# Recurrence and expert layer on one core: reordered first steps, and the last four tiles' lists built in two parts

## The chip, the cores and the metric

The kernel runs on one core of one Trainium2 chip. The metric is the device time of one execution in microseconds (us), the median of several runs. The engines are TensorE (PE; its weight loads are a row of their own, PEld), VectorE (DVE), ScalarE (ACT), GpSimd (POOL) and SyncE (SP), which here only issues transfers. Each works through its own instructions in order; the program fixes that order, and an instruction that waits holds all that stand behind it on its engine.

## What is computed

A recurrence over 768 positions for 4 batches of 8 heads of width 48, and then a layer of 8 experts on the 3072 rows that it gives:

```python
for t in range(S):
    cur = einsum('bhd,bhe->bhde', u * k[t], v[t])
    y[t] = einsum('bhd,bhde->bhe', r[t], state + cur)
    state = w * state + einsum('bhd,bhe->bhde', k[t], v[t])
x = y as rows (3072 x 384)
do_compute = x @ w_skip > 0
logits = x[do_compute] @ w_gate          # 8 experts
e_idx = argmax(logits); gate = softmax(logits)[e_idx]
out[row] = x[row] + gate * (relu(x[row] @ w1[e]) @ w2[e])   # rows not chosen: x
```

## The kernel before, in words

**The recurrence** runs in 24 steps n = 0 to 23: two pairs of batches, 12 steps each, every step 64 positions of two batches. A step's r is multiplied by a table of powers of w (`prep_r`, on VectorE), its k by a table of inverse powers (`prep_k`, mostly on POOL); a second copy of r, the bonus, carries u (`bonus`: one part per pair of heads on ScalarE, or a half at once on another engine). There are four such tables, `w_d[0..3]`; `grow(1)`, `grow(2)`, `grow(3)` make the later ones from the first. On TensorE a step is `scores` (k times r), `within` (masked scores times v), `turn_x` and `turn_k` (transposes), `state` and `across`. `mask_scores(n)` copies the scores out of the bank `ps_p` in two VectorE operations; the scores of step n+1 go into the same bank. `warm` puts matmuls without use on TensorE while it has nothing else. `blank` zeroes the part of a v tile that a block-diagonal product needs empty.

`load_rk(n)` brings r and k of a step, `load_v` its v. All loads are issued by SP, except `ub` and k of step 0, which ScalarE issues. The order of the first steps is written out by hand (lines 959 to 981).

**Routing.** A step's 128 rows are a tile. Gating gives each tile 9 logits in `lg`; tiles 0 to 22 are gated by fours (`gate_four`, `gate_back`), tile 23 alone (`gate`, line 692). `route` turns the logits of a group of tiles into lists, for each expert, of row numbers and weights: groups (0, 8), (8, 16), (16, 20) and (20, 24). On VectorE it finds the maximum, the choice `oh`, the weight; on TensorE the ranks (line 770 and on), which need `oh`; on VectorE two operands `ol` and `vl`; on TensorE the list matmuls (line 842). Their result is added to `lists`; `place` makes the index `gid` from it, and `gather` brings the rows of the output that the index names, by a DMA from POOL. There are 16 slots of rows: slot 0 to 7 the first 128 rows of each expert, slot 8 to 15 up to 104 more. Slot 8 is the first one that the last group's lists are needed for.

**From attention to the experts.** Expert 0's slot 0 is worked on while the last steps run, by the generator `single` (called `first`; line 198): three groups of widening matmuls for one half of the hidden layer (line 218), then the other half, `flip` (transposes and a copy), `narrow` (line 247) and `rest` (the low part, on VectorE). `run(k)` lets it go on by k pieces. After the last step come lines 1077 to 1087: one piece, the gating of tile 23, the routing of the last group up to its choice, two pieces, the ranks and the operands, two pieces, lists and index; then the gathers. Slot 8 is the next slot that TensorE turns, while it still works on slot 0. After that, experts 1 to 7 follow in `expert`.

Of the kernel before, what the change touches and what calls it, by code (L numbers as in the profile page):

```python
# [9 lines left out]
F32 = mybir.dt.float32  # L10
F32R = mybir.dt.float32r
# [11 lines left out]
P = 128  # L23
# [38 lines left out]
def tile_wkv_moe(  # L62
# [135 lines left out]
    def single(q, w1, w2, xhl, made, ph, pt, py, turned=False):  # L198
# [69 lines left out]
        if turned:  # L268
            rest(0)
            narrow(0, 1, parts=(0,))  # L270
            yield
            flip(1)
            narrow(2, 3, parts=(0,))
            narrow(0, 1, 2, 3, parts=(1,))
            rest(1)
        else:
            narrow(0, 1)
            yield
            flip(1)
            rest(1)  # L280
            narrow(2, 3)
# [12 lines left out]
    with ExitStack() as actx:  # L294
# [34 lines left out]
        def load_rk(n):  # L329
            d = ld.tile([DR, 2, NB * NHP * C], F32, tag="dm", name=f"dm{n}", bufs=3)  # L330
            for eng, s in ((nc.sync, slice(0, 1)), (nc.scalar, slice(1, 2))) if n == 0 else ((nc.sync, slice(0, 2)),):
                eng.dma_start(
                    out=d[:, s].rearrange("p s (q c) -> p s q c", c=C), in_=dm[n // NSTEP, n % NSTEP, :, s]
                )
            loaded[n] = (d, v_of(n))
# [377 lines left out]
        def route(g0, g1):  # L713
# [4 lines left out]
            def near(w=None):  # L718
                if g1 == NT:
                    free[0] += 1  # L720
                    return small(f"near{free[0]}", w=w, bufs=1)
                a = free[0]
# [25 lines left out]
            nc.vector.tensor_tensor(df, l8, bc(mx), ALU.subtract)  # L748
            if g1 == NT:
                nc.scalar.activation(df, df, AF.Exp)  # L750
            yield 0
            if g1 < NT:
                nc.scalar.activation(df, df, AF.Exp)
            nc.vector.tensor_tensor(eq[:, :, :E], eq[:, :, :E], rdo, ALU.mult)
# [72 lines left out]
            if late:  # L827
                nc.vector.tensor_tensor(
                    ol, lane1[:, None, :].to_broadcast([P, n, P]), r1.unsqueeze(2).to_broadcast([P, n, P]), ALU.is_equal
                )  # L830
                ohp = oh
                if g1 < NT:
                    ohp = near(E)
                    nc.vector.tensor_copy(ohp, oh)
                vl = small("vl", F32R, NV3 * E)
# [10 lines left out]
                nc.vector.tensor_tensor(last, part[:, :, NJ - 1, :], last, ALU.add)  # L846
                if g1 < NT:
                    count()
                    nc.vector.tensor_tensor(before, before, sums, ALU.add)
                else:  # L850
                    place(1)
                nc.vector.tensor_scalar(over[:, g0:g1], r1, float(CAP), None, ALU.is_ge)
# [39 lines left out]

        def place(j):
            c = slice(j * E, (j + 1) * E)
            ids = lists[:, 0, j]
            nc.vector.tensor_scalar(gid[:, c], ids, 1.0, 0.0, ALU.subtract, ALU.max)
            em2 = sm.tile([P, E], F32, tag="em2", name=f"em2{j}")
# [71 lines left out]
        square(8, nc.gpsimd)  # L969
        k1 = prep_k(1, after=prep_r(1))  # L970
        for j in range(2, 4):
            blank(j, nc.gpsimd)
        bonus(1, (0, 1, 2, 3))
        mask_scores(0)
        warm(3, ps_t)
        state(0)
        warm(2, ps_t)
        grow(2, nc.vector)
        prep_k(2, after=prep_r(2))
        bonus(2, (0, 1, 2, 3))  # L980
        grow(3, nc.gpsimd)

# [90 lines left out]
        def run(k):  # L1073
            for _ in range(k):
                next(first, None)

        run(1)
        gate(NT - 1)
        assert not routes
        last = route(ends[NT], NT)  # L1080
        while next(last) == 0:
            pass
        run(2)
        while next(last) == 0:
            pass
        run(2)
        both(last)
# [341 lines left out]
```

## Time and profile before

| | us |
|---|---|
| median of 3 runs | 266.14 |
| lowest and highest run | 264.6, 269.08 |
| profiled execution, its own time | 263.44 |
| span of the profiled execution, first to last instruction | 261.7 |
| mean granted TensorE clock | 0.996 |
| TensorE busy in the span | 252.4 (96%) |
| VectorE, ScalarE, POOL busy | 169.6, 139.0, 112.6 |

Times in the trace count from the start of the span. The steps of the recurrence fill the first 115 us or so, the experts the time from about 136 us on. Busy shares are means over stretches with different limits; what a change is worth is read from the waits in its own stretch.

### The profile page before, as it was taken

How to read it: one execution, taken by the hardware profiler on the slowest of the kernel's cores; microseconds unless marked ns; L12 is line 12 of the kernel's file. 1: busy time of each engine (PE TensorE's matmuls, PEld its weight loads, DVE VectorE, ACT ScalarE, POOL GpSimd, SP SyncE). 2: the span in 40 equal slices, each digit the busy share in tenths (PEclk: the TensorE clock that was granted, in tenths of full speed). 3: DMA queues.
4: the chain of work that ended last, by engine and by line, in shares of the span. 5: the costliest groups of instructions: out<-in, count | busy, mean ns of one | idle time of the engine just before them, and what ended most of it. 6: DMA issues, size and time to landing. Idle time of an engine off the chain costs nothing.

```text
span 261.7 us, 8596 instructions
## 1 busy us (share of the span) xinstructions
PE 252.4 (96%) x3578; PEld 225.2 (86%) x3580; DVE 169.6 (65%) x381; ACT 139.0 (53%) x315; POOL 112.6 (43%) x130
## 2 busy tenths in 40 slices
PE   7999999999999999999999999999999999999990
PEld 2688888888887888778699999999999999999990
DVE  7867547579554696638873797858569387494300
ACT  2655766667656664635753837539167273490200
POOL 7679647476646836202887061310501303105011
PEclk9999999999999999999999999999999999999998
DMA  6998699989998688695499959394390760001000
GB/s 170 252 248 253 207 259 257 270 223 277 234 255 230 170 261 272 146 326 182 130 301 294 324 168 367 114 357 170 100 407 13 260 271 29 19 0 40 7 33 24
DMA packets 20704, 51.82 MB, mean 198 GB/s; under 512 B 3540, under 2 KB 9952, under 8 KB 20656
## 3 DMA queue, kind: packets, MB, share of 16 engines
q1 hardware_dynamic: 18352, 45.81, 58.6%
q0 software_dynamic: 2048, 5.14, 6.3%
q8 instruction: 30, 0.49, 0.8%
q10 hardware_dynamic: 256, 0.23, 0.3%
q14 instruction: 18, 0.15, 0.2%
HBM read 43.77 MB, written 7.96 MB: 198 GB/s over the span
## 4 chain that ended last, share of the span: by engine, by line
PE 95%; DMA 1%; issue 1%; DVE 1%; POOL 0%; POOLq 0%; ACT 0%
PE ps_p L179 11%; PE ps_y L179 11%; PE ps_p L533 9%; PE ps_y L587 8%; PE ps_s L557 7%; PE ps_p L169 5%; PE ps_y L169 5%; PE ps_x L169 5%; PE ps_l L169 5%; PE ps_y L603 5%; PE ps_t L657 4%; PE ps_l L519 3%; PE ps_t L304 3%; PE ps_t L674 2%; PE ps_y L247 2%; PE ps_l L218 2%
## 5 line engine op out<-in xcount | busy, mean ns | idle before, releaser
L188 POOL DMA_INDIRECT out_dram<-xg,sid x16 | 24.8, 1550 | 88.3 <-DVE xg L184 78.4
L130 DVE TENSOR_TENSOR wlo<-raw,whi 128x512 fp32r<-128x512 f32 x84 | 53.9, 683 | 1.3 <-ACT h L222 0.7
L125 ACT CAST whi<-raw 128x512 fp32r<-128x512 f32 x96 | 54.7, 627 | 0.0
L506 POOL TENSOR_TENSOR kd<-dm,w_d 112x512 f32<-112x512 f32 x23 | 29.3, 1275 | 2.1 <-DVE rd L481 2.0
L139 POOL DMA_INDIRECT xg<-out_dram,gid x16 | 19.2, 1200 | 20.0 <-DVE em L898 15.7
L481 DVE TENSOR_TENSOR rd<-dm,w_d 112x512 f32<-112x512 f32 x24 | 17.3, 722 | 14.9 <-PE ps_y L603 14.0
L533 PE MATMUL ps_p<-rd,kd 48*64 48x128 f32 x768 | 26.8, 274 | 0.0
L491 POOL TENSOR_TENSOR rd<-rd,uw 112x256 f32<-112x256 f32 x21 | 12.9, 613 | 30.5 <-DVE rd L481 15.3
L533 PEld LDWEIGHTS ps_p<-rd,kd 48*64 48x64 f32 x768 | 21.1, 133 | 2.6 <-issue 1.2
L545 DVE COPY_PREDICATED am<-below,ps_p 128x512 f32<-128x512 int8 x24 | 17.7, 737 | 6.7 <-PE ps_p L533 6.3
L587 PE MATMUL ps_y<-vkv,am 128*64 128x96 f32 x384 | 21.4, 253 | 0.6 <-issue 0.6
L499 ACT ACTIVATE rd<-rd,uw 112x128 f32<-112x128 f32 x52 | 17.9, 396 | 7.3 <-DVE rd L481 7.1
L661 ACT COPY x<-ps_t 128x384 f32<-128x384 f32 x23 | 11.0, 479 | 19.1 <-PE ps_t L657 19.0
L587 PEld LDWEIGHTS ps_y<-vkv,am 128*64 128x64 f32 x384 | 16.7, 136 | 4.9 <-issue 3.5
L173 ACT ACTIVATE hh<-ps_p 128x464 fp32r<-128x464 f32 x7 | 3.9, 558 | 31.1 <-PE ps_p L169 31.1
L179 PE MATMUL ps_p<-whi,hh 128*128 128x384 f32 x56 | 19.4, 347 | 0.0
L557 PE MATMUL ps_s<-vkv,kt 128*48 128x96 f32 x352 | 19.1, 251 | 0.0
L179 PE MATMUL ps_y<-whi,hh 128*104 128x384 f32 x56 | 18.9, 338 | 0.0
L179 PE MATMUL ps_y<-wlo,hh 128*104 128x384 f32 x56 | 18.9, 337 | 0.0
L179 PE MATMUL ps_p<-whi,hl 128*128 128x384 f32 x56 | 18.9, 337 | 0.0
L179 PE MATMUL ps_y<-whi,hl 128*104 128x384 f32 x56 | 18.9, 337 | 0.0
L179 PE MATMUL ps_p<-wlo,hh 128*128 128x384 f32 x56 | 18.9, 337 | 0.0
(244 smaller groups left out, 610.6 us busy)
## 6 DMA issues: line engine op xcount, KB each, us to landing
raw<-in_w_dram SPq DMA_DIRECT2D x16, 768.0 KB
dm<-in_dm_dram SPq DMA_DIRECT2D x23, 448.0 KB
raw<-in_w_dram SPq DMA_DIRECT2D x24, 256.0 KB
raw<-in_w_dram SPq DMA_DIRECT2D x12, 512.0 KB
out_dram<-xt SPq DMA_DIRECT2D x24, 192.0 KB
vkv<-in_tok_dram SPq DMA_DIRECT2D x22, 192.0 KB
vkv<-in_tok_dram SPq DMA_DIRECT2D x4, 96.0 KB
out_dram<-xt SPq DMA_DIRECT2D x4, 96.0 KB
```

The lines of the kernel that those rows point to most:

```text
L125: nc.scalar.copy(wsp[e][0][:, s], raw[e][:, s])
L130: eng.tensor_tensor(lo[:, s], raw[e][:, s], hi[:, s].bitcast(F32), ALU.subtract)
L139: ins = nc.gpsimd.indirect_dma_start(out=xg[:m], out_offset=None, in_=out[:rows], in_offset=bass.IndirectOffsetOnAxis(ap=gid[:m, q : q + 1 ...
L169: nc.tensor.matmul(ph, w1[a][:, c, fs], x[:, c, b, :], start=(k == 0), stop=(k == 3 * NCC - 1))
L179: nc.tensor.matmul(py, a, b[:, f, :], start=(k == 0), stop=(k == 3 * NFC - 1))
L188: ins = nc.gpsimd.indirect_dma_start(out=out, out_offset=bass.IndirectOffsetOnAxis(ap=sid[:m, q : q + 1], axis=0), in_=xs.pop(q)[:m], in_o ...
L499: nc.scalar.activation(rd[:, :, hp, 1], rd[:, :, hp, 0], AF.Copy, scale=uw[:, hp : hp + 1])
L506: ins = (eng or nc.gpsimd).tensor_tensor(kds[n].rearrange("p b h c -> p b (h c)")[:, part], d[:, part], table.to_broadcast([DR, part.stop ...
L533: mm = nc.tensor.matmul(ps_p[g * C : (g + 1) * C, a, j * P : (j + 1) * P], kd[h, b, hp, :], rd[h, b, hp].rearrange("p s c -> p (s c)"), st ...
L545: nc.vector.copy_predicated(shape(am[n % 2]), below, p[:, :, 0])
L557: nc.tensor.matmul(s[a * C : a * C + D, j * 2 * D : (j + 1) * 2 * D], kt[:, j, a, :], v[:, j, a], start=i == 0 and j == 0, stop=True, skip ...
L587: nc.tensor.matmul(ps_y[b * C : (b + 1) * C, a, jj * 2 * D : (jj + 1) * 2 * D], am[n % 2][:, a, j * C : (j + 1) * C], v[:, j, a], start=jj ...
```

## The change

Four edits. (1) k of step 0 is issued by SP, right behind r, and no longer by ScalarE. (2) In the first three steps the bonus of steps 1 and 2 is made half by ScalarE and half by VectorE; the table of step 2 and k of step 2 come ahead of the mask of step 0; the two blocks that POOL zeroes stand apart; two of the five warming matmuls go. (3) The last group's routing is a function of its own, `route_end`. It chooses, ranks and spreads tiles 20 to 22 ahead of the gating of tile 23, then tile 23 alone, and makes the index straight from the bank in which the list matmuls leave their sums, ahead of the addition to `lists`. (4) `single` has one pause fewer, so that the first narrowing matmuls come behind the list matmuls. `route` loses the branches that only the last group used.

```diff
@@ single
         if turned:
             rest(0)
             narrow(0, 1, parts=(0,))
-            yield
             flip(1)
@@ load_rk
-            for eng, s in ((nc.sync, slice(0, 1)), (nc.scalar, slice(1, 2))) if n == 0 else ((nc.sync, slice(0, 2)),):
-                eng.dma_start(
+            for s in (slice(0, 1), slice(1, 2)) if n == 0 else (slice(0, 2),):
+                nc.sync.dma_start(
@@ route_end (new)
+            def choose(a, b):
+                q, l8, m = slice(a, b), lg[:, g0 + a : g0 + b, 0:E], b - a
+                nc.vector.tensor_reduce(mx[:, q], l8, AX.X, ALU.max)
+                nc.vector.scalar_tensor_tensor(rdo[:, q], ..., ALU.is_gt, ALU.mult)
+                nc.vector.tensor_tensor(eq[:, q, :E], l8, bc(mx[:, q]), ALU.is_equal)
+                nc.vector.tensor_tensor(df[:, q], l8, bc(mx[:, q]), ALU.subtract)
+                nc.scalar.activation(df[:, q], df[:, q], AF.Exp)
+                nc.vector.tensor_tensor(eq[:, q, :E], eq[:, q, :E], rdo[:, q], ALU.mult)
+                nc.vector.tensor_reduce(m2[:, q], eq[:, q], AX.X, ALU.max)
+                nc.vector.tensor_tensor(oh[:, q], eq[:, q, :E], bc(m2[:, q]), ALU.is_equal)
+            def rank(a, b):
+                nc.tensor.matmul(cols(0), tri, oh[:, a:b].rearrange(col), start=True, ...)
+                more = [(0, before[:, None, :].to_broadcast([P, m, E]))]
+                more += [(j, oh[:, a : b - j].rearrange(col)) for j in range(1, m)]
+                more += [(0, oh[:, j : j + 1].to_broadcast([P, m, E])) for j in range(a)]
+                for k, (j, x) in enumerate(more):
+                    nc.tensor.matmul(cols(j), ones[:, :P], x, start=False, ...)
+            def spread(a, b):
+                # on VectorE: sum of df, value of the row number, 1e-9, reciprocal, rank product,
+                # gh, its sum r1, gl, ol, value of gh, value of gl
...
+            choose(0, n - 1)
+            yield
+            rank(0, n - 1)
+            spread(0, n - 1)
+            nc.vector.tensor_scalar(ids1, lists[:, 0, NJ - 1], 1.0, 0.0, ALU.subtract, ALU.max)
+            yield
+            choose(n - 1, n)
+            yield
+            rank(n - 1, n)
+            spread(n - 1, n)
+            yield
+            for j in range(n):
+                nc.tensor.matmul(part, ol[:, j, :], vl[:, j, :], start=(j == 0), stop=(j == n - 1))
+            nc.vector.scalar_tensor_tensor(gid[:, E : 2 * E], part[:, 0], 1.0, ids1, ALU.subtract, ALU.max)
+            nc.vector.tensor_tensor(last, part, last, ALU.add)
+            place(1, False)
@@ the first steps
-        k1 = prep_k(1, after=prep_r(1))
-        for j in range(2, 4):
-            blank(j, nc.gpsimd)
-        bonus(1, (0, 1, 2, 3))
+        blank(2, nc.gpsimd)
+        prep_k(1, after=prep_r(1))
+        bonus(1, (0, 1))
+        bonus(1, (2, 3), nc.vector)
+        grow(2, nc.vector)
+        prep_k(2)
+        grow(3, nc.gpsimd)
+        blank(3, nc.gpsimd)
         mask_scores(0)
         warm(3, ps_t)
         state(0)
-        warm(2, ps_t)
-        grow(2, nc.vector)
-        prep_k(2, after=prep_r(2))
-        bonus(2, (0, 1, 2, 3))
-        grow(3, nc.gpsimd)
+        prep_r(2)
+        bonus(2, (0, 1))
+        bonus(2, (2, 3), nc.vector)
@@ behind the last step
+        assert not routes
+        last = route_end(ends[NT])
+        next(last)
         run(1)
+        next(last)
         gate(NT - 1)
-        assert not routes
-        last = route(ends[NT], NT)
-        while next(last) == 0:
-            pass
+        next(last)
         run(2)
-        while next(last) == 0:
-            pass
-        run(2)
+        next(last)
+        run(1)
         both(last)
```

## Rows read from the trace of the kernel before

**Rows 1.** The page's part 4, shares of the chain by engine.

```profile
PE 95%; DMA 1%; issue 1%; DVE 1%; POOL 0%; POOLq 0%; ACT 0%
```

**Rows 2.** The chain, first 20 us: start, length (us), engine, tile, line, count.

```profile
10.23 0.54 PE ps_t L304 x2
10.77 1.03 PE ps_p L533 x32
...
13.54 1.10 PE ps_p L533 x32
```

**Rows 3.** Timeline, first 12 us: start, length, engine, line, operation, idle before.

```profile
1.25 0.45 ACTq L332 DMA_DIRECT2D dm<-in_dm_dram  x1
...
4.93 0.16 DVE L428 TENSOR_TENSOR uw<-ub_sb,pw 112x4 f32<-112x4 f32 x1
...
5.40 0.69 DVE L481 TENSOR_TENSOR rd<-dm,w_d 112x512 f32<-112x512 f32 x1 [0.32 <-DMA dm<-in_dm_dram]
...
6.01 0.43 DVE L506 TENSOR_TENSOR kd<-dm,w_d 112x256 f32<-112x256 f32 x1
...
6.37 0.43 DVE L491 TENSOR_TENSOR rd<-rd,uw 112x256 f32<-112x256 f32 x1
...
7.06 0.68 DVE L397 TENSOR_TENSOR w_d<-w_d,pw 112x512 f32<-112x512 f32 x1
...
7.77 0.69 DVE L481 TENSOR_TENSOR rd<-dm,w_d 112x512 f32<-112x512 f32 x1
...
8.38 0.72 DVE L545 COPY_PREDICATED am<-below,ps_p 128x512 f32<-128x512 int8 x1
8.54 1.27 POOL L506 TENSOR_TENSOR kd<-dm,w_d 112x512 f32<-112x512 f32 x1 [2.03 <-DVE rd L481]
...
9.16 1.28 ACT L499 ACTIVATE rd<-rd,uw 112x128 f32<-112x128 f32 x4
...
11.87 0.74 DVE L545 COPY_PREDICATED am<-below,ps_p 128x512 f32<-128x512 int8 x1 [0.62 <-PE ps_p L533]
```

**Rows 4.** The chain from 106 to 128 us.

```profile
116.52 0.76 PE ps_y L697 x6
117.28 1.47 PE ps_l L218 x6
118.75 0.09 PE ps_x L770
...
120.12 0.95 PE ps_p L247 x4
...
121.46 0.19 DVE lists L846
...
121.67 0.17 DVE gid L896
...
122.15 2.96 DMA xg<-out_dram,gid
```

**Rows 5.** Timeline from 105 us on, ScalarE and VectorE at the last routing.

```profile
115.12 0.19 ACT L689 COPY lg<-ps_t 128x27 f32<-128x27 f32 x1
...
115.98 0.06 DVE L733 MEMSET near<- 128x4 f32 x1
...
117.52 0.19 DVE L735 TENSOR_REDUCE near<-lg 128x4 f32<-128x32 f32 x1 [1.48 <-ACT lg L704]
...
118.42 0.19 DVE L759 TENSOR_TENSOR oh<-near,m 128x32 bf16<-128x32 f32 x1
...
119.04 0.16 DVE L798 TENSOR_TENSOR rkp<-ps_x,oh 128x32 f32<-128x32 f32 x1
...
120.42 0.18 DVE L837 TENSOR_TENSOR vl<-oh,gl 128x32 fp32r<-128x32 bf16 x1
```

**Rows 6.** Timeline from 123.5 us on, TensorE at the gathered rows of slot 8.

```profile
125.33 0.49 PE L160 MATMUL ps_s<-ident,xg 104*128 104x104 f32 x3 [0.62 <-DMA xg<-out_dram,gid]
```

**Rows 7.** Stretch: length, TensorE busy (instructions), granted clock, DMA share, GB/s.

```profile
124.70:125.40 0.70, 0.08 (x2) 1.00 0.01 4
```

More of the change, by code (lines that the diff above doesn't have):

```diff
@@ L718, in near @@
             def near(w=None):
-                if g1 == NT:
-                    free[0] += 1
-                    return small(f"near{free[0]}", w=w, bufs=1)
                 a = free[0]
@@ L748, in route @@
             nc.vector.tensor_tensor(df, l8, bc(mx), ALU.subtract)
-            if g1 == NT:
-                nc.scalar.activation(df, df, AF.Exp)
             yield 0
-            if g1 < NT:
-                nc.scalar.activation(df, df, AF.Exp)
+            nc.scalar.activation(df, df, AF.Exp)
             nc.vector.tensor_tensor(eq[:, :, :E], eq[:, :, :E], rdo, ALU.mult)
@@ L830, in route @@
                 )
[L831 to L834, printed above, removed]
+                ohp = near(E)
+                nc.vector.tensor_copy(ohp, oh)
                 vl = small("vl", F32R, NV3 * E)
@@ L846, in route @@
                 nc.vector.tensor_tensor(last, part[:, :, NJ - 1, :], last, ALU.add)
[L847 to L851, printed above, removed]
+                count()
+                nc.vector.tensor_tensor(before, before, sums, ALU.add)
                 nc.vector.tensor_scalar(over[:, g0:g1], r1, float(CAP), None, ALU.is_ge)
@@ L894, in place @@
+        def place(j, given=True):
             c = slice(j * E, (j + 1) * E)
             ids = lists[:, 0, j]
-            nc.vector.tensor_scalar(gid[:, c], ids, 1.0, 0.0, ALU.subtract, ALU.max)
+            if given:
+                nc.vector.tensor_scalar(gid[:, c], ids, 1.0, 0.0, ALU.subtract, ALU.max)
             em2 = sm.tile([P, E], F32, tag="em2", name=f"em2{j}")
```

58 lines of the change are left out of this document (57 added, 1 removed).

## The prediction

> **What bounds the kernel now.** I read the chain of work that ended last first, because it says which engine a saved microsecond has to come from. TensorE holds 95% of it [rows 1]. So a delay or an advance of TensorE arrives, nearly whole, at the end, and a gain on another engine counts only where TensorE waits for it. The change touches two places where it might: the first three steps, and the passage from attention to the experts.
>
> In the first place I read the chain of the first microseconds, then the timeline of all engines beside it. The scores of step 1 start at 10.77, behind two warming matmuls of 0.54 us that start at 10.23 [rows 2]. They also need the bonus of step 1, whose four ScalarE parts end at 9.16 + 1.28 = 10.44, and the mask of step 0, since VectorE reads the scores of step 0 out of the same bank [rows 3].
>
> In the second place the chain runs through TensorE until the lists at 121.46, then through the index (121.67) and a gather that starts at 122.15 and takes 2.96 us [rows 4]. The timeline of TensorE has the other side of it: 0.62 us idle, from 124.71, until the gathered rows came [rows 6]. That is all that an earlier gather can give back; before and after it TensorE itself is the chain.
>
> **The first steps.** VectorE works in order. From t, the start of the first r product (5.40), the timeline gives: k's first half at +0.61, table of step 1 at +1.66, r of step 1 at +2.37, first mask at +2.98 [rows 3]. The change puts two operations ahead of that mask: half a bonus and the table of step 2. A half operation takes 0.345 us from start to start (two of them from 6.37 to 7.06), a table 0.71 (7.06 to 7.77) where the next reads it and 0.61 where it doesn't, as r to mask (7.77 to 8.38). The half bonus reads what r's product just wrote, so 0.71 stands between these. The mask starts at 2.37 + 0.71 + 0.345 + 0.61 = t + 4.04.
>
> What t becomes is not in the trace. VectorE sat idle for 0.32 us until r had landed; its operation before ends at 4.93 + 0.16 = 5.09 [rows 3], the lower end, and the old 5.40 is the upper. I take 5.09: the k that ScalarE sent at the same time is as large as r, and it now stands behind r, so only r's own half of that traffic is left ahead. The mask then starts at 9.13. From the second mask to the scores behind it there are 13.54 - 11.87 = 1.67 us [rows 2, 3], so the scores of step 1 start at 10.80: **+0.03 us**. With t = 5.40 it is +0.34. Less than nothing I exclude: the table operations keep VectorE until 5.09 whatever lands, and the rest is VectorE's own work.
>
> The other edits here cost nothing, under this cover. Two bonus parts instead of four leave ScalarE done near 9.85, a microsecond ahead of the scores. POOL fills one block in the 2.03 us in which it waited for r of step 1 [rows 3]; then k of step 1, k of step 2, a table and the other block follow each other. By 1.27 us for each k, k of step 2 ends about 10.9, before the scores of step 1 are over; without that cover it could cost step 2 its start, which is 13.54. The two warming matmuls that go leave 0.6 us of pause. Such a pause did not lower the clock: in 124.70 to 125.40, with TensorE busy for 0.08 of 0.70 us, the granted clock was 1.00, the upper level of 2.4 GHz [rows 7]. The later loads leave SP 0.45 us later, which is the length of ScalarE's issue [rows 3]; only the first r was waited for, and of the loads behind it only the first k is needed within a microsecond (below).
>
> **The passage.** Routing of tiles 20 to 22 is put ahead of the last gating matmul, and TensorE is in order too. VectorE is free for it after a fill at 115.98 + 0.06; the logits of the three tiles are there at 115.12 + 0.19 [rows 5]. The maximum starts at about 116.06. From there to the end of the choice the trace has 118.42 + 0.19 - 117.52 = 1.09 us for four tiles [rows 5]; these operations last 0.06 to 0.2 us whatever they hold, so I take the same for three. The choice is there at 117.15, and for TensorE, with 0.1 us for the signal, at 117.25. TensorE is done with widening at 116.52, where gating starts today [rows 4]. **First wait: 0.73 us**, with the gating (0.76, from 116.52 to 117.28) queued behind it, and behind the gating the routing of tile 23. The ranks of three tiles are four small matmuls, 0.17 us (an estimate: the first of the ranks at 118.75 takes 0.09, the others less). Gating ends at 117.25 + 0.17 + 0.76 = 118.18, the six widening matmuls (1.47, 117.28 to 118.75 [rows 4]) at 119.65.
>
> VectorE meanwhile does the rest for tiles 20 to 22. Rank product to last value took 120.42 - 119.04 = 1.38 us [rows 5]; with the index values ahead of the ranks now, three tiles instead of four in the widest operation, and one operation more for the old index, I count 1.17. The product starts at about 117.60, so the maximum of tile 23 starts at 118.77. Its choice ends 1.09 later and reaches TensorE at 119.96. **Second wait: 0.31 us.** Ranks, turning and the last widening take 120.12 - 118.75 = 1.37 us [rows 4], until 121.33; VectorE's last value is ready near 121.21 and holds nothing.
>
> The list matmuls (from 120.12 + 0.95 to 121.46, 0.39) end at 121.72. The index now comes right there, without the 0.21 us of the sum ahead of it; with 0.48 us from index to gather (121.67 to 122.15 [rows 4]) the gather starts at 122.20, and its rows are there 3.18 later as today, at 125.38. TensorE asks for them after the narrowing matmuls (0.95), now behind the lists, and the 3.25 us that lie between 121.46 and 124.71: 121.72 + 0.95 + 3.25 = 125.92. So the old wait is gone and nothing waits for the gather, but TensorE is at this point 125.92 - 125.33 = **+0.59 us** late: 0.73 + 0.31 + 0.17 - 0.62. ScalarE's relus now stand behind an exponential and come 0.3 us later; what reads them runs after 120. The remainder of the first hidden half moves behind the lists on VectorE, and its reader on TensorE moves with it. Bounds: without either wait 0.17 - 0.62 = -0.45; with each of VectorE's eighteen small operations 0.05 us longer, half way to the 0.2 of dependent ones, +0.59 + 0.9 = +1.5.
>
> **Sum**: +0.03 + 0.59 = +0.62 us, 264.1 against the profiled execution's 263.44 (span 261.7). The runs shown have a median of 266.14, 2.7 above it, so the prediction is 266.14 + 0.62 = 266.8.
>
> **The rivals.** *k comes late.* It leaves SP behind r. Its first half was read at 6.01, so it had landed by then; 0.45 us later is 6.46 at worst, against a need at 5.09 + 0.61 = 5.70 [rows 3]. That moves VectorE's whole chain by 0.76: +0.79 at the scores, +1.38 in all, 267.5. Against it: r and k are the first large loads either way, and nothing shares with them now. The Trainium skill ("DMA: Bandwidth & Descriptors", section "Issuing engines are not separate DMA queues") says that starting transfers from several engines saves only the sequencer's time to start them; by that rule this is the case to fear, since that time is lost here, and no row shows when k landed.
>
> *The passage gains*, the ending on the other side. If the choice of three tiles is there when TensorE asks, the gather's 0.62 us is what counts. It decides where both new waits together stay under 0.62 - 0.17 - 0.03 = 0.42 us. With half of that the sum is -0.21, 265.9; with none -0.42. For it: only one tile's work is left behind the gating. Against it: VectorE is free at 116.04 and needs 1.09 us, and TensorE asks at 116.52 [rows 4, 5].
>
> *Nothing comes of it*: the waits cost what the gather gives back, +0.1, 266.2. For it: each of the terms is small; against it, their sum was worked out one by one and has one sign.
>
> **How the numbers follow.** Forecast 0.5, late k 0.15, gain 0.2, nothing 0.15. The cases lie from -0.42 to +1.38, that is 265.7 to 267.5; the runs of one kernel lie themselves between 264.6 and 269.08, so I widen by 1.1 us to each side: 264.6 to 268.6. Two per cent, about what a measurement of this kernel can tell from no change, is 5.3 us, and every case lies inside; 0.02 faster and 0.03 slower are left for what I don't see. Same 0.95.
>
> **What would show it.** TensorE waiting for VectorE's choice near 116.5, and again, shorter, near 119.7; the gather at about 122.2 and no wait for it; the mask of step 0 near 9.1, the scores of step 1 near 10.8, and the first r product starting near 5.1. The forecast is wrong if TensorE doesn't wait for the choice, if the scores of step 1 start before 10.5, or if the gather still holds TensorE.

## The result, and the profile after

| | before | after |
|---|---|---|
| median, us | 266.1 (20 runs) | 267.17 (20 runs) |
| lowest run, us | 263.63 | 264.97 |
| profiled execution, its own time, us | 263.44 | 266.51 |
| span of the profiled execution, us | 261.7 | 264.7 |
| mean granted TensorE clock in it | 0.996 | 0.988 |

The ratio of after to before is 1.0068, with a 95% interval of 1.0043 to 1.0092. (The comparison leaves disturbed executions out, so it isn't the ratio of the two medians.) On 266.1 us that is +1.8 us, between 1.1 and 2.4: within 2%, as forecast, and inside the range of 264.6 to 268.6. But the forecast's own difference, +0.62 us or 1.0023, lies below the interval. The two profiled executions are 3.0 us apart in span. So the figure came near and its reasons have to be looked at one by one.

The chain that ended last is still TensorE's, but less so. This is the page's part 4 of after, which answers to [rows 1]:

```profile
PE 90%; DVE 4%; DMA 2%; SPq 0%; issue 0%; POOL 0%; POOLq 0%; ACT 0%; DVEq 0%
```

TensorE held 95% before. VectorE and transfers now hold 6% of it. Where, the chain of the first microseconds says, in order of time (start us, us, what); it answers to [rows 2]:

```profile
2.18 6.20 DMA dm<-in_dm_dram
...
8.48 0.70 DVE rd L480
...
9.63 1.68 DVE w_d L396
11.30 0.65 DVE am L544
...
12.85 2.02 PE ps_p L532 x32
...
17.23 1.03 PE ps_p L532 x32
```

Until 12.71 us TensorE is not in this chain at all. The chain runs through a load, then through r of step 1, half a bonus, the table of step 2 and the two masks of step 0, all on VectorE. The scores of step 1 start at 12.85 (10.77 before; forecast 10.80) and last 2.02 us instead of 1.03, and the scores of step 2 start at 17.23 instead of 13.54 [rows 2]. The timeline of the same microseconds (start us, us, engine, line, operation, out<-in, and in brackets the idle time before it with what ended it) answers to [rows 3]:

```profile
5.04 0.69 DVE L480 TENSOR_TENSOR rd<-dm,w_d 112x512 f32<-112x512 f32 x1
5.66 0.42 DVE L505 TENSOR_TENSOR kd<-dm,w_d 112x256 f32<-112x256 f32 x1
...
6.70 0.68 DVE L396 TENSOR_TENSOR w_d<-w_d,pw 112x512 f32<-112x512 f32 x1
8.48 0.69 DVE L480 TENSOR_TENSOR rd<-dm,w_d 112x512 f32<-112x512 f32 x1 [1.10 <-DMA dm<-in_dm_dram]
9.20 0.42 DVE L490 TENSOR_TENSOR rd<-rd,uw 112x256 f32<-112x256 f32 x1
9.30 1.45 POOL L505 TENSOR_TENSOR kd<-dm,w_d 112x512 f32<-112x512 f32 x1 [1.99 <-DVE rd L480]
9.54 1.76 DVE L396 TENSOR_TENSOR w_d<-w_d,pw 112x512 f32<-112x512 f32 x1
11.23 0.71 DVE L544 COPY_PREDICATED am<-below,ps_p 128x512 f32<-128x512 int8 x1
...
12.59 0.87 DVE L480 TENSOR_TENSOR rd<-dm,w_d 112x512 f32<-112x512 f32 x1
...
12.88 1.49 POOL L396 TENSOR_TENSOR w_d<-w_d,pw 112x512 f32<-112x512 f32 x1
13.50 1.15 DVE L490 TENSOR_TENSOR rd<-rd,uw 112x256 f32<-112x256 f32 x1
```

Two things stand here that [rows 3] doesn't have. r of step 1 waits 1.10 us for its load, and starts at 8.48; the forecast had it at 5.09 + 2.37 = 7.46. And the table of step 2 takes 1.76 us, where the table of step 1 in the same execution takes 0.68. It started 0.24 us after POOL's product for k of step 1 and ended 0.55 us after that product's end (11.30 against 10.75). From its start to the mask behind it 1.69 us pass, where the forecast had 0.61: 1.08 more. With the load's 1.02 this is 2.10, exactly the mask's 11.23 less the 9.13 of the forecast. The last three lines show two smaller cases of the same kind: r of step 2 takes 0.87 us instead of 0.69, and its half bonus 1.15 instead of 0.42, each beginning while POOL multiplies (its k of step 2 from 11.65 to 12.91, then its table of step 3).

What came next was a fall of the clock. The busy time of each engine in stretches of after (length; busy us of PE, PEld, DVE, ACT, POOL with counts; granted clock; share of the transfer engines; GB/s):

```profile
10.40:12.80 2.40, 0.00 (x0) 0.00 (x0) 2.37 (x4) 0.48 (x1) 1.50 (x2) 1.00 1.04 201
12.80:14.80 2.00, 1.95 (x34) 1.65 (x34) 1.81 (x2) 0.70 (x2) 1.95 (x4) 0.50 1.14 218
14.80:16.40 1.60, 1.51 (x19) 1.32 (x18) 1.48 (x3) 0.05 (x1) 0.38 (x1) 0.56 1.05 207
16.40:18.30 1.90, 1.84 (x39) 1.45 (x40) 0.55 (x1) 1.47 (x4) 1.20 (x2) 1.00 1.03 226
```

TensorE does nothing for 2.4 us; then its granted clock is 0.50, that is 1.2 GHz instead of 2.4, for some 3.6 us. The scores of step 1 take 1.0 us longer by it and what follows up to the scores of step 2 another 0.62: before, 13.54 - 11.80 = 1.74 us passed from the end of the one to the start of the other, after, 17.23 - 14.87 = 2.36, since the products of step 0 take 1.55 us instead of 0.88. So 2.08 for the late start, 0.99 and 0.62 make the 3.69 us by which step 2 is late. How much of the last two the clock alone would cost, e6 shows below.

The passage from attention to the experts answers to [rows 4, 6]. The last step's transposes in the timeline of before, just ahead of [rows 4]:

```profile
115.28 0.55 PE L657 MATMUL ps_y<-ident,xt 128*128 128x128 f32 x3
```

The timeline of TensorE in after, with the index and the gather:

```profile
118.24 0.55 PE L656 MATMUL ps_y<-ident,xt 128*128 128x128 f32 x3
...
120.01 0.17 PE L922 MATMUL ps_x<-ohe,tri 128*128 128x24 bf16 x1 [0.52 <-DVE ohe L917]
122.53 0.17 PE L922 MATMUL ps_x<-ohe,tri 128*128 128x8 bf16 x1
124.37 0.17 DVE L973 SCALAR_TENSOR_TENSOR gid<-ps_x,ids 128x8 uint32<-128x8 f32 x1 [0.69 <-PE ps_x L971]
124.84 1.08 POOL L139 DMA_INDIRECT xg<-out_dram,gid  x1 [13.36 <-DVE em L984]
124.97 0.60 PE L233 MATMUL ps_t<-ident,h 128*128 128x128 f32 x4
128.22 0.49 PE L160 MATMUL ps_s<-ident,xg 104*128 104x104 f32 x3
```

From the last step's transposes to those of slot 8 there were 125.33 - 115.28 = 10.05 us before [rows 6]; now there are 128.22 - 118.24 = 9.98. TensorE waits for the choice as foretold, and its matmuls don't wait for the gather any more. The net is nothing, where +0.59 was forecast. All of the loss in these two executions lies in the first 18 us. Of the 3.69 us 0.7 have come back by step 23 (its transposes are 2.96 late), in part through pauses of TensorE without a named cause that differ from trace to trace (0.56 us at 79.45 before, 0.30 at 77.28 after); from there to the end the distance stays at 2.9 to 3.0.

### The profile page after: what moved, and what is told of

Same layout as the page of the kernel before. It is cut to its first block, busy times and chain, and to the rows that moved or that the text cites. A ratio compares the mean times of both kernels' runs of the same rounds, so it can differ in the third digit from the quotient of the medians.

```text
span 264.7 us, 8617 instructions
## 1 busy us (share of the span) xinstructions
PE 252.5 (95%) x3580; PEld 226.6 (86%) x3582; DVE 172.6 (65%) x402; ACT 138.2 (52%) x312; POOL 111.1 (42%) x130
## 4 chain that ended last, share of the span: by engine, by line
PE 90%; DVE 4%; DMA 2%; SPq 0%; issue 0%; POOL 0%; POOLq 0%; ACT 0%; DVEq 0%
PE ps_p L179 11%; PE ps_y L179 11%; PE ps_p L532 9%; PE ps_y L586 7%; PE ps_s L556 6%; PE ps_p L169 5%; PE ps_y L169 5%; PE ps_x L169 5%; PE ps_l L169 5%; PE ps_y L602 5%; PE ps_t L656 4%; PE ps_l L518 3%; DMA dm<-in_dm_dram 2%; PE ps_t L673 2%; PE ps_p L247 2%; PE ps_y L247 2%
## 5 line engine op out<-in xcount | busy, mean ns | idle before, releaser
L188 POOL DMA_INDIRECT out_dram<-xg,sid x16 | 23.3, 1458 | 90.1 <-DVE xg L184 79.8
L480 DVE TENSOR_TENSOR rd<-dm,w_d 112x512 f32<-112x512 f32 x24 | 16.7, 697 | 14.5 <-PE ps_y L602 13.4
L532 PEld LDWEIGHTS ps_p<-rd,kd 48*64 48x64 f32 x768 | 21.7, 137 | 4.5 <-issue 3.4
L586 PE MATMUL ps_y<-vkv,am 128*64 128x96 f32 x384 | 22.0, 257 | 0.0
L498 ACT ACTIVATE rd<-rd,uw 112x128 f32<-112x128 f32 x48 | 16.7, 397 | 9.3 <-DVE rd L480 9.2
L586 PEld LDWEIGHTS ps_y<-vkv,am 128*64 128x64 f32 x384 | 17.4, 140 | 4.4 <-issue 2.9
```

The costliest lines, as they stand in the source:

```text
L188: ins = nc.gpsimd.indirect_dma_start(out=out, out_offset=bass.IndirectOffsetOnAxis(ap=sid[:m, q : q + 1], axis=0), in_=xs.pop(q)[:m], in_o ...
L480: ins = nc.vector.tensor_tensor(rd[:, :, :, 0], d, w_d[:, n % NSUB, 0][:, None].to_broadcast([DR, NB, NHP, C]), ALU.mult)
L532: mm = nc.tensor.matmul(ps_p[g * C : (g + 1) * C, a, j * P : (j + 1) * P], kd[h, b, hp, :], rd[h, b, hp].rearrange("p s c -> p (s c)"), st ...
L586: nc.tensor.matmul(ps_y[b * C : (b + 1) * C, a, jj * 2 * D : (jj + 1) * 2 * D], am[n % 2][:, a, j * C : (j + 1) * C], v[:, j, a], start=jj ...
```

## The experiments

The ratios are against the kernel before, timed in the same rounds on the same chip. The variants come from four such groups on four chips, so two variants of different groups, or a variant and after, are compared only through their ratios.

| run | what it is | ratio [95%] | scores of step 1 / 2 start at, us |
|---|---|---|---|
| | the kernel after | 1.0068 [1.0043, 1.0092] | 12.85 / 17.16 |
| e2 | passage alone | 0.9992 [0.9951, 1.0033] | as before |
| e13 | passage alone, on another chip | 1.0021 [0.9987, 1.0055] | as before |
| e3 | first steps alone | 1.0063 [1.0022, 1.0104] | 12.48 / 16.72 |
| e1 | after, k of step 0 on ScalarE again | 1.0057 [1.0017, 1.0097] | 12.17 / 16.50 |
| e4 | after, mask ahead of the table | 1.0038 [0.9992, 1.0084] | 10.81 / 14.92 |
| e5 | after, table ahead of r of step 1 | 1.0001 [0.9941, 1.0061] | 10.39 / 13.82 |
| e10 | after, POOL's k behind the table | 1.0102 [1.0047, 1.0156] | 11.39 / 14.79 |
| e6 | after, ten warming matmuls more | 1.0067 [1.0019, 1.0116] | 12.57 / 15.73 |
| e9 | before, k of step 0 on SP | 1.0014 [0.9956, 1.0072] | 10.39 / 13.29 |
| e8 | before, bonus of step 1 halved | 1.0031 [0.9988, 1.0075] | 10.76 / 13.59 |
| e11 | before, table ahead of r of step 1 | 1.0036 [0.9996, 1.0075] | 10.99 / 13.82 |
| e12 | e2 with the gating ahead of the ranks | 1.0061 [1.002, 1.0102] | not changed |

Starts are those of the timeline, where before has 10.70 and 13.54. Two accounts of the first steps were set against each other. One puts the loss on the loads: k on SP's queue makes what stands behind it late. The other puts it on the order of VectorE: the table ahead of the mask, and what the table meets there.

### Which of the two places

**e2** undoes the first steps and keeps the passage; **e13** is the same kernel again, on another chip some 45 minutes later. **e3** is the kernel before with the new first steps alone.

```diff
@@ e2, against after
-            for s in (slice(0, 1), slice(1, 2)) if n == 0 else (slice(0, 2),):
-                nc.sync.dma_start(
+            for eng, s in ((nc.sync, slice(0, 1)), (nc.scalar, slice(1, 2))) if n == 0 else ((nc.sync, slice(0, 2)),):
+                eng.dma_start(
...
-        prep_k(1, after=prep_r(1))
-        bonus(1, (0, 1))
-        bonus(1, (2, 3), nc.vector)
-        grow(2, nc.vector)
-        prep_k(2)
...
+        bonus(1, (0, 1, 2, 3))
...
+        grow(2, nc.vector)
+        prep_k(2, after=prep_r(2))
...
```

> The kernel after with its first steps and the k of step 0 put back as they were; only the last routing in two parts, the index ahead of the sum and the moved narrowing are left. Theory (the loss is in the first steps, the passage is neutral): within 0.3 us of the kernel before, ratio 0.999 to 1.001, and TensorE waits about 0.5 and 0.2 us for the two choices while the wait for the gather (0.62 us) is gone. Rival (the passage costs what was forecast and the first steps only lost by an accident of one execution): +0.6 us, ratio about 1.002.

> The kernel before with only the new first steps (k of step 0 from SP, halves of the bonus, table and k of step 2 ahead of the mask); the last routing is the old one. Theory (the loss is in the first steps): the whole of the change's ratio of 1.007, +1.5 to +2.5 us; the table of step 2 takes about 1.7 us on VectorE beside POOL's k of step 1, and the scores of step 1 start after 11.5 us. Rival (an accident): within 0.4 us of before, scores of step 1 near 10.8.

> The new passage alone on the old first steps once more, the same kernel as in the first experiment, on another chip and day. The traces of both orders of the passage reach the gathered rows 9.95 to 10.07 us after the last transposes of attention, but the version with the gating first was timed at 1.006. Theory (the passage is neutral and single series of some ten runs differ by half a per cent by chance): ratio between 0.996 and 1.004, and again 9.9 to 10.1 us in the trace. Rival (the passage costs 0.5% or more that one series missed): ratio above 1.004.

The passage alone can't be told from the kernel before by its ratio, twice. From transposes to slot 8 it takes 125.52 - 115.57 = 9.95 us in e2 and 128.40 - 118.43 = 9.97 in e13, against 10.05. The first steps alone give 1.0063, as much as the whole change. In e3's trace r of step 1 waits 0.72 us for its load, the table of step 2 takes 1.76 us, and the granted clock is 0.52 from 13.6 to 17.0 us.

By the traces the loss is in the first steps: step 2 starts 3.2 us late in e3 and on time in e2 and e13. The timing agrees but doesn't prove it: the intervals of e3 and e13 overlap, and e12 below, with the old first steps, was timed at 1.0061. Nor does the span of one profiled execution decide: e13's is 264.7 us, as long as after's, with nothing lost in the first steps but two of TensorE's unnamed pauses (1.31 and 1.12 us) further on.

### Loads or order

**e1** puts k of step 0 back on ScalarE, and changes nothing else of after.

```diff
-            for s in (slice(0, 1), slice(1, 2)) if n == 0 else (slice(0, 2),):
-                nc.sync.dma_start(
+            for eng, s in ((nc.sync, slice(0, 1)), (nc.scalar, slice(1, 2))) if n == 0 else ((nc.sync, slice(0, 2)),):
+                eng.dma_start(
```

> The kernel after with k of step 0 issued by ScalarE again, all else as after. Theory A (the load order costs: loads behind k leave SP 0.45 us later, so r of step 1 lands later): 0.4 to 1.0 us faster than after, the product of r of step 1 waits less than 0.5 us for its load. Theory B (the order of VectorE's work costs, not the loads): no more than 0.3 us from after, +1.5 us over before, and the table of step 2 still takes about 1.7 us.

The timeline of e1:

```profile
5.43 0.69 DVE L480 TENSOR_TENSOR rd<-dm,w_d 112x512 f32<-112x512 f32 x1 [0.35 <-DMA dm<-in_dm_dram]
7.79 0.69 DVE L480 TENSOR_TENSOR rd<-dm,w_d 112x512 f32<-112x512 f32 x1
8.62 1.46 POOL L505 TENSOR_TENSOR kd<-dm,w_d 112x512 f32<-112x512 f32 x1 [1.26 <-DVE rd L480]
8.86 1.76 DVE L396 TENSOR_TENSOR w_d<-w_d,pw 112x512 f32<-112x512 f32 x1
12.17 1.95 PE L532 MATMUL ps_p<-rd,kd 48*64 48x128 f32 x32 [2.15 <-DVE am L545]
```

Without k on SP's queue, r of step 0 waits again (0.35 us, 0.32 in [rows 3]) and r of step 1 doesn't. All else stays: the table takes 1.76 us beside POOL, TensorE waits 2.15 us, and its clock falls (0.54 in 12 to 15 us). The ratio stays too. The load costs 0.68 us at the scores of step 1 (12.85 - 12.17) between these two traces; e3 and e6, where r of step 1 waits 0.72 and 0.81 us, start at 12.48 and 12.57, which makes it 0.3 to 0.4. The timing doesn't resolve it.

**e4** leaves the loads as in after and puts the mask of step 0 ahead of the table again.

```diff
+        mask_scores(0)
         grow(2, nc.vector)
         prep_k(2)
         grow(3, nc.gpsimd)
         blank(3, nc.gpsimd)
-        mask_scores(0)
```

> The kernel after with the mask of step 0 put back ahead of the table of step 2 on VectorE; k of step 0 stays on SP, the half bonus stays. Theory B (the table ahead of the mask costs, 0.7 us of its own and 1.0 of being held while POOL multiplies): 1.0 to 2.0 us faster than after, scores of step 1 start 1.7 us or more earlier relative to the product of r of step 1, TensorE's pause before them is under 1 us and the granted clock stays at 1.00. Theory A (the loads): within 0.4 us of after.

The timeline of e4:

```profile
8.87 1.46 POOL L505 TENSOR_TENSOR kd<-dm,w_d 112x512 f32<-112x512 f32 x1 [1.56 <-DVE rd L480]
9.11 0.73 DVE L544 COPY_PREDICATED am<-below,ps_p 128x512 f32<-128x512 int8 x1
10.56 0.68 DVE L396 TENSOR_TENSOR w_d<-w_d,pw 112x512 f32<-112x512 f32 x1
11.31 1.78 POOL L505 TENSOR_TENSOR kd<-dm,w_d 112x512 f32<-112x512 f32 x1 [0.99 <-DVE w_d L396]
11.99 1.38 DVE L490 TENSOR_TENSOR rd<-rd,uw 112x256 f32<-112x256 f32 x1
14.92 1.10 PE L532 MATMUL ps_p<-rd,kd 48*64 48x128 f32 x32 [1.27 <-DVE am L545]
```

Three things are to be seen. The mask runs beside the same POOL product and isn't held: 0.73 us. The table, now behind POOL's product, takes its 0.68. And the scores of step 1 start at 10.81, the old time, though r of step 1 waits 0.67 us for its load in e4 too. But k of step 2, which POOL makes as soon as its table is there, now meets the half bonus of step 2, which takes 1.38 us where the first half bonus takes 0.42; so step 2 starts at 14.92 and not at 13.54. The stall has moved on by one step. TensorE's pauses of 0.96 and 1.27 us leave its granted clock at 1.00 (10 to 18 us). The ratio is lower, though not told apart from after's.

**e10** leaves the table where after has it and makes POOL wait for it with k of step 1.

```diff
@@ grow
+                return ins
@@ the first steps
-        prep_k(1, after=prep_r(1))
+        prep_r(1)
...
-        grow(2, nc.vector)
+        prep_k(1, after=grow(2, nc.vector))
```

> The kernel after with POOL's k of step 1 made to wait for the table of step 2; VectorE's order is untouched. Theory (held while POOL multiplies): the table takes 0.7 us, the first mask starts 1.0 us sooner behind the product of r, and the scores of step 1 start about 1 us sooner although k of step 1 is later; 0.5 to 1.5 us faster than after. Rival (the table has its own slowness): table 1.7 us, the scores of step 1 about 0.7 us later than in the kernel after since k comes later.

The timeline of e10:

```profile
9.17 0.68 DVE L396 TENSOR_TENSOR w_d<-w_d,pw 112x512 f32<-112x512 f32 x1
9.77 0.72 DVE L545 COPY_PREDICATED am<-below,ps_p 128x512 f32<-128x512 int8 x1
9.99 2.96 POOL L506 TENSOR_TENSOR kd<-dm,w_d 112x512 f32<-112x512 f32 x2 [2.68 <-DVE w_d L396]
11.39 1.10 PE L533 MATMUL ps_p<-rd,kd 48*64 48x128 f32 x32 [1.46 <-POOL kd L506]
```

This is the plain test. The same table in the same place, with POOL still, takes 0.68 us instead of 1.76, and the mask comes at 9.77 instead of 11.23 (0.38 us of this is the load, since r of step 1 starts at 8.10 here and at 8.48 in after). TensorE now waits for POOL, but its scores start 1.46 us sooner than after's and last 1.10; the granted clock stays at 1.00 behind the pause of 1.46 us. By the trace it had to be faster than after. By the timing it is the slowest of all, 1.0102. Its profile has unnamed pauses of TensorE of 0.52, 0.74 and 0.39 us, which doesn't settle it. That the product holds the table is shown; that removing this pays was not.

**e5** moves the table of step 2 ahead of r of step 1, where POOL has nothing to multiply.

```diff
+        grow(2, nc.vector)
         prep_k(1, after=prep_r(1))
         bonus(1, (0, 1))
         bonus(1, (2, 3), nc.vector)
-        grow(2, nc.vector)
```

> The kernel after with the table of step 2 moved one place up on VectorE, ahead of the product of r of step 1, so that it runs before POOL can start k of step 1. Theory (VectorE's two-input operations are held while POOL multiplies): the table takes 0.7 us instead of 1.76, the mask of step 0 starts 0.9 us or more sooner behind the product of r of step 1, and the half bonus of step 2, which still meets POOL's table, stays above 1 us; 0.5 to 1.5 us faster than after. Rival (the table of step 2 is slow for a reason of its own, its operands or its tile): it takes 1.7 us here too and the kernel is within 0.3 us of after.

The timeline of e5:

```profile
6.47 1.30 DVE L396 TENSOR_TENSOR w_d<-w_d,pw 112x512 f32<-112x512 f32 x2
7.69 0.68 DVE L480 TENSOR_TENSOR rd<-dm,w_d 112x512 f32<-112x512 f32 x1
...
10.39 1.10 PE L532 MATMUL ps_p<-rd,kd 48*64 48x128 f32 x32 [0.41 <-DVE am L545]
```

Both tables together take 1.30 us, and the second of them fills the time in which VectorE would have waited for r of step 1. The scores of step 1 come at 10.39, ahead of before. The half bonus of step 2 still meets POOL's k of step 2 (1.38 us), and the scores of step 2 come at 13.82 (13.54 before). The ratio is 1.0001 with six runs: after's loss is gone in the estimate, though the interval, 0.9941 to 1.0061, overlaps after's.

### The clock by itself

**e6** is after with ten more warming matmuls in the pause.

```diff
         warm(3, ps_t)
         state(0)
+        warm(10, ps_t)
```

> The kernel after with ten matmuls without use behind the state of step 0, about 2.2 us, so that TensorE doesn't pause before the scores of step 1. Theory (the pause of 2.5 us brought the granted clock to half, which doubled the scores and the products of step 1): granted clock 1.00 throughout the first 20 us, scores of step 1 in 1.03 us instead of 2.02, 0.7 to 1.5 us faster than after. Rival (the slow scores came from something else, or VectorE and POOL set the pace anyway): less than 0.3 us from after.

Busy time by stretches in e6, with the columns of above:

```profile
10.00:13.00 3.00, 2.73 (x27) 1.31 (x30) 2.96 (x4) 0.48 (x1) 2.37 (x3) 1.00 1.06 216
```

And the timeline of e6, the scores of steps 1 and 2 and the half bonus of step 2:

```profile
12.57 1.10 PE L532 MATMUL ps_p<-rd,kd 48*64 48x128 f32 x32 [0.27 <-DVE am L545]
...
13.03 1.15 DVE L490 TENSOR_TENSOR rd<-rd,uw 112x256 f32<-112x256 f32 x1
...
15.73 1.10 PE L532 MATMUL ps_p<-rd,kd 48*64 48x128 f32 x32 [0.32 <-DVE am L545]
```

With TensorE busy the granted clock stays at 1.00 in the first 20 us, the scores take 1.10 us instead of 1.98, and step 2 starts at 15.73 instead of 17.16. So the pause is what brought the clock down. From the scores of step 1 to those of step 2 there are 15.73 - 12.57 = 3.16 us in e6, 17.16 - 12.85 = 4.31 in after and 13.54 - 10.70 = 2.84 before: the clock is worth 1.15 us, and 0.32 are lost at full clock too, where the half bonus of step 2 is held (1.15 us) and TensorE waits for the mask behind it.

The slow clock isn't a peculiarity of one execution either: over the executions compared, the median of the mean granted clock is 0.989 to 0.991 in after, e1 and e3, the three kernels with the pause of more than 2 us, and 0.993 to 0.997 in the other ten; before has 0.992 to 0.996 in its four groups. Yet e6 is not faster than after in timing (1.0067 and 1.0068). Six runs leave room, since its interval goes down to 1.0019, but the 1.4 us by which step 2 starts sooner should have shown in part. This stays open.

### Parts alone

**e9** is before with k of step 0 on SP; **e8** is before with the bonus of step 1 half on VectorE and without the two warming matmuls; **e11** is before with the table as in e5, the halved bonus, the parted blocks and no second warming.

```diff
@@ e8, against before
-        bonus(1, (0, 1, 2, 3))
+        bonus(1, (0, 1))
+        bonus(1, (2, 3), nc.vector)
         mask_scores(0)
         warm(3, ps_t)
         state(0)
-        warm(2, ps_t)
@@ e11, against before
-        k1 = prep_k(1, after=prep_r(1))
-        for j in range(2, 4):
-            blank(j, nc.gpsimd)
-        bonus(1, (0, 1, 2, 3))
+        grow(2, nc.vector)
+        blank(2, nc.gpsimd)
+        prep_k(1, after=prep_r(1))
+        bonus(1, (0, 1))
+        bonus(1, (2, 3), nc.vector)
...
-        warm(2, ps_t)
-        grow(2, nc.vector)
         prep_k(2, after=prep_r(2))
         bonus(2, (0, 1, 2, 3))
         grow(3, nc.gpsimd)
+        blank(3, nc.gpsimd)
```

> The kernel before with nothing but k of step 0 issued by SP behind r. Theory A (loads behind k come later): the first product of r starts at 5.05 instead of 5.4, but the product of r of step 1 waits for its load until about 8.0 to 8.4, and the kernel is 0.2 to 0.6 us slower than before. Theory B (the load order is harmless by itself): within 0.2 us of before, scores of step 1 at 10.8 or earlier.

> The kernel before with one part of the change: the bonus of step 1 is half ScalarE's and half VectorE's, and the two warming matmuls behind the state of step 0 go. Nothing that VectorE does ahead of the mask meets POOL's multiplication there except the half bonus, a one-tensor product that ends about when POOL starts. Theory (only the table and the half bonus of step 2 were held): half bonus 0.43 us, scores of step 1 near 10.5 instead of 10.77, within 0.4 us of before. Rival (any extra work of VectorE ahead of the mask costs): scores of step 1 after 11.0 and 0.5 us or more slower.

> The kernel before with the table of step 2 ahead of the product of r of step 1 (before POOL multiplies), the half bonus of step 1 on VectorE, no second warming, and, unlike the kernel after, k of step 2 still behind r of step 2 and the whole bonus of step 2 on ScalarE; k of step 0 stays on ScalarE, the last routing is the old one. Theory (holding is all that was wrong with the new order): no VectorE operation of the first 14 us is longer than 0.8 us, scores of step 1 before 11.2, those of step 2 near 13.5, within 0.5 us of before and 1 us or more faster than the kernel after. Rival (the table is too early at any place ahead of the mask): scores of step 2 after 14.3, 0.8 us or more slower than before.

None of the three is told apart from before. In e9 r of step 0 starts at 5.05 without a wait, r of step 1 waits 0.55 us, and the scores of step 1 come at 10.46 by the chain (10.77 before). In e8 the mask starts at 9.06 and the scores at 10.76: half a bonus on VectorE costs nothing there, as forecast, and behind a pause of 0.55 us the granted clock stays at 1.00 (10.8 to 14 us). In e11 the tables take 1.28 us together, no VectorE operation of the first steps is held, and the profiled execution is the shortest of all kernels here (263.04 us, span 261.2); the timing, 1.0036, still doesn't put it ahead of before.

e9 also shows a thing that can explain scatter between executions. Busy time by stretches in e9:

```profile
18.00:19.00 1.00, 0.00 (x0) 0.00 (x0) 0.00 (x0) 0.00 (x0) 0.00 (x0) 1.00 1.09 200
...
20.00:23.00 3.00, 3.00 (x37) 2.45 (x30) 2.16 (x4) 0.66 (x3) 2.81 (x6) 0.50 0.76 149
```

And TensorE's timeline in e9 at the end of the first stretch:

```profile
19.18 0.33 PE L603 MATMUL ps_y<-sblk,rd 48*64 48x48 f32 x7 [1.79 <-issue]
```

TensorE stood for 1.79 us and waited for nothing that the profile shows. VectorE stood at the same time, but for a load of its own (r of a later step waited 2.98 us, until 19.24), ScalarE for TensorE and POOL for VectorE. The granted clock was 0.50 afterwards. A pause of this kind, 0.3 to 1.8 us, stands in each of the fourteen traces. Their places aren't wholly free: seven traces have one within the scores at 74 to 78 us (0.28 to 1.12 us), four within those at 23 to 25 us (0.52 to 1.72).

### The order in the passage

**e12** is e2 with the gating of tile 23 ahead of the ranks of the other three tiles, so that the first wait has nothing to hold.

```diff
         run(1)
-        next(last)
         gate(NT - 1)
         next(last)
+        next(last)
```

> The passage of the kernel after on the old first steps, with the gating of tile 23 put back ahead of the ranks of tiles 20 to 22. Theory (TensorE's two new waits and the gather's old one trade one to one): the first wait (0.52 us) goes, the second grows from 0.2 to about 0.6 us, and the experts begin within 0.3 us of where they begin with the ranks first, counted from the last transposes of attention. Rival (the first wait is a pure loss): the second wait stays at 0.2 us and the experts begin 0.5 us sooner.

The timeline of TensorE in e12:

```profile
117.46 0.17 PE L922 MATMUL ps_x<-ohe,tri 128*128 128x24 bf16 x1
119.92 0.17 PE L922 MATMUL ps_x<-ohe,tri 128*128 128x8 bf16 x1 [0.71 <-DVE ohe L917]
125.57 0.45 PE L160 MATMUL ps_s<-ident,xg 104*128 104x104 f32 x3
```

The first wait is gone and the second has grown to 0.71 us, about as much as the two together had been; from 115.60 to 125.57 the passage takes 9.97 us, as in e2. VectorE's row of small operations is what sets the second choice, and TensorE waits for it in one place or in two. The timing (1.0061, against 0.9992 and 1.0021 for e2's kernel) says something else, and no row of the trace bears it out: the profiled executions of e2 and e12 both have a span of 262.1 us. Half a per cent between such series can't be trusted here.

## Why the prediction was right or wrong

**t and the first k: right.** The r product started at 5.04 (5.09 forecast). k's first half was read at 5.66 without a wait, so the rival in which it comes late fell. One place fell with it: "of the loads behind it only the first k is needed within a microsecond". The next load, r and k of step 1, is needed 2.4 us after t, and in the kernels with k on SP it landed 0.55 to 1.10 us too late (after, e3, e4, e6, e9, e10), but for e5, where the second table fills that time; with k on ScalarE r of step 1 doesn't wait (e1). SP's queue had gained a transfer ahead of it, and the forecast had counted that as 0.45 us of issue and stopped there. The sentence of the Trainium skill that the forecast weighed ("DMA: Bandwidth & Descriptors", section "Issuing engines are not separate DMA queues") named the sequencer's time as all that several issuing engines save. The traces agree that such time is lost, and that it is felt one load later than feared.

**The table: the step that failed.** The price of a table, 0.71 us where the next operation reads it and 0.61 where it doesn't, was read from rows where POOL had no product of its own running, and the order of the change put it beside one. There it took 1.76 us: +1.08 on the path. e10 shows the cause by the same table in the same place with POOL still (0.68), and e3 and e1 that neither the passage nor the moved k is needed for it. The mask, one of whose sources is the bank `ps_p`, isn't held by the same product (e4). That it is the two sources in SBUF which make the difference fits all these traces, but no run changed the source alone. [rows 3] had a pair that is not held, the mask beside POOL's k, and none that is; the forecast named no way in which POOL could hold VectorE. The Trainium skill has the rule ("GPSIMD Engine Reference", section "Specifications"): GpSimd shares its interfaces to SBUF with VectorE and contends with VectorE's instructions that have two SBUF inputs. The traces agree: 1.76 us beside POOL's product, 0.68 without.

The kernel before held a hint. `prep_k(2, after=prep_r(2))` made POOL start behind r, which kept this pair apart in step 2. The change dropped it, and r of step 2 met POOL's k (0.87 us in after). The half bonus of step 2, new on VectorE, met POOL's table of step 3 in after (1.15 us) and POOL's k in e4 (1.38).

**The clock: wrong through the size of the pause.** That a pause of 0.6 us doesn't lower it holds (e8, [rows 7]). But the pause became 2.46 us, because the mask was late, and after it the granted clock was 0.50 for 3.6 us. The forecast named no way in which a late mask would cost more than its lateness. Besides the 2.08, 1.6 us more were lost in the profiled execution until step 2 started; by e6 about 1.15 of them are the clock's, and the rest mostly the held half bonus.

**The passage: right in kind, the sum wrong.** Both waits came where they were put, so the rival "the passage gains" fell; the gather was no longer waited for; and "nothing comes of it" is what happened. By stretches: to the second ranks +0.91 us, where 1.21 was forecast (120.01 and 122.53 stand 1.77 and 4.29 behind the transposes; forecast 1.97 and 4.68). The waits were 0.52 and about 0.25 us for 0.73 and 0.31. The first choice began 0.10 us sooner than forecast and took 1.04 us for 1.09, the second 0.96 for 1.09, and the signal to TensorE, put at 0.1 us, took 0.05. From there to the second flip -0.17, where nothing was forecast, because the stretch counted as TensorE's work held a wait of TensorE's own. It stands in the timeline of the weight loads of before:

```profile
120.10 0.19 PEld L247 LDWEIGHTS ps_p<-whi,hh 128*128 128x128 f32 x1 [0.42 <-ACT hh L234]
```

In after the list matmuls fill that time, and no such wait is left. From the flip to slot 8 -0.81, where -0.62 was forecast: the end of a matmul in a trace is modelled, and the next starts before it where nothing is waited for (0.17 us from start to start, 0.34 long), so the old wait was worth up to 0.17 more than its 0.62. The sum is -0.07 instead of +0.59.

**The median: near by two errors.** The first steps were to cost 0.03 us and cost far more; the passage was to cost 0.59 and cost nothing. What is left of the 3.0 us between the profiled executions in the timed comparison is 1.8. The profiled execution of before was one of its shorter ones (263.44 against a median of 266.1).

**What stays open.** That POOL's product holds the table, and that the long pause lowers the clock, is shown. That these make up the 1.8 us of the timed comparison is not: e10 and e6, whose traces are better than after's, aren't timed faster than it, and e12 is timed slower than e2. Open too is what TensorE's unnamed pauses are. That its instructions come late while the transfer engines are full (the share is above 1.00 around e9's pause) would fit, but is only argued. No kernel that was run is told to be faster than before: e2 and e5 come nearest, and their intervals hold 1.

## What to carry to other kernels

Before an operation with two SBUF inputs is moved on VectorE, look at what POOL multiplies at that time in the new order: here the pair cost 1.1 us, about what was left of POOL's product when the table began, and a dependence written as "behind" may be what keeps such a pair apart. When a load is moved to another queue, follow the loads behind it to their first readers, not only the one that moves. And price a delay ahead of TensorE by the pause that it makes as well: here one of 2.46 us cost some 1.2 us more through the slower clock behind it, and behind one of 0.55 us the clock didn't fall.

## What the runs showed of the hardware

- A VectorE product of two SBUF operands (112x512, 0.68 us) took 1.76 us where it began while a POOL product of two such operands was running, and ended 0.55 us behind it. A half bonus (112x256, 0.43 us) took 1.15 to 1.38 in that place and ended 0.28 us behind POOL. So the price is about what is left of POOL's operation. The mask with a PSUM source kept its 0.72 us.
- The one that began first kept its time: the half bonus of step 1 began 0.10 us ahead of POOL's product and took its 0.42 us, and the product took 1.45 or 1.46 us instead of 1.27, with the held table beside it (after) or without (e4, e5, e11).
- After a pause of TensorE of 2.46 us its granted clock was 0.50 (1.2 GHz) for about 3.6 us; after pauses of 0.55 us (e8) and 1.46 us (e10) it stayed at 1.00 (2.4 GHz).
- TensorE pauses of 0.3 to 1.8 us with nothing waited for stand in all fourteen traces, half of them with one within the scores at 74 to 78 us, and a long one takes the clock down too (1.79 us in e9, then 0.50 over 3 us).
